# Ten of sixteen input tiles read in transposed form and normalised with broadcast rows, instead of being transposed on TensorE

## The chip, the cores and the metric

The kernel runs on one core of a Trainium2 chip. A core has five engines that run side by side: TensorE (PE in the profile, with PEld for its weight loads), VectorE (DVE), ScalarE (ACT), GpSimd (POOL) and SyncE (SP, which here only issues transfers). Each has its own instruction queue, worked off in order; they meet by semaphores. Transfers between DRAM and the on-chip memory run on 16 DMA engines, and a queue that issues one goes on at once unless the next instruction has to wait. PE writes into PSUM, eight banks of 128x512 words here. The metric is the device time of one execution in microseconds (us).

## The reference

S = 2048 rows, D = 512, F = 1792. Everything is float32.

```python
xn = layernorm(x)
# A: 32 heads of 16, each row looks at 8 rows, 2 apart, behind it
q, k, v = split(xn @ wqkv)                        # 512 -> 3*512
s = softmax(q . k[window] * 16**-0.5) @ v[window] @ wo
# B: a gated MLP with a spatial product
z = gelu(xn @ w_in)                               # 512 -> 1792
z1, z2 = z[:, :896], layernorm(z[:, 896:])
g = w_sp @ z2 + b_sp[:, None]                     # 2048 x 2048 over the rows
b = (z1 * g) @ w_out                              # 896 -> 512
out = x + s * silu(b)
```

## The kernel before

Row r of x is p*16 + j: tile j (0 to 15) holds rows p*16 + j, with p on the 128 partitions. Every matrix product is computed in three: both operands are split into a high part (fp32r, a rounded copy made by ACT) and a low part (source minus high, made by DVE), and PE adds hi·hi, hi·lo and lo·hi. So one 128x512 result over 512 channels takes 4 blocks x 3 = 12 products of 512 columns.

The stages on PE, in order:

1. Warm-up and opening. `keep_warm` (L191) multiplies the identity while the first loads run. `opening` (L196) fixes by hand the order of tiles 0 to 5: loads, layernorm statistics (`stats_x`, L160: DVE bn_stats and aggregate, plus eps, GpSimd power -1/2), normalisation (`normal_x`, L167, on rows), four PE transposes of 128x128 into one bank (`turned_x`, L170, L173), the high copy by ACT (L174) and the low part by DVE (`low_x`, L177). The normalised, transposed tile is what the qkv products read, and later z1 and z2.
2. qkv in three groups of 512 output columns, g = 0, 1, 2, each 16 tiles x 12 products (`product`, L266; in the opening `times`, L208). From tile 6 on, `layernorm_in(j + 1)` (L181) makes the next tile while tile j is multiplied. ACT copies each result into a stage buffer (L303), and a pair of tiles is written to DRAM (qkv_d, L310).
3. z1: 7 blocks of columns x 4 chunks c of rows (L398 to L410), chunk c being tiles 4c to 4c + 3; gelu by ACT at the eviction (L409), written to DRAM.
4. z2: 16 tiles x 2 halves h of 512 and 384 columns (L420 to L444), gelu (L432), layernorm statistics and split on DVE (L436, L441).
5. g: 4 chunks of rows x 16 tiles x 7 blocks (L469 to L478), with w_sp split on the way (wsp, L137); evictions with the bias and the gate z1 (L498 to L514).
6. The end: final weights wout and wo and the gated u (ul) are loaded and split (L481 to L489), then b (7 blocks, 21 products per tile) and s, and the output.

Attention (`attention`, L323) is DVE work beside PE's stages 2 to 5, in eight subs of four heads; sub 0 needs q, k, v blocks 0 to 2, which all lie in group 0. It has the lowest priority. The final weights lie in attention's memory, so their loads follow its end.

The order of each engine's instructions is made when the kernel is built, by a scheduler that plays the program through; what `pin` names is kept in the order it is written in (the opening, the weights, the layernorm of x). SP's queue holds nearly all loads, ACT's the writes of qkv, z1 and g.

Of the kernel before, what the change touches and what calls it, by code (L numbers as in the profile page):

```python
# [10 lines left out]
F32 = mybir.dt.float32  # L11
# [29 lines left out]
WARM = 10  # L41
OPEN = 6
TCKW = {"schedule_with_timeline_sim": True}
# [3 lines left out]
def kernel(  # L47
    ctx: ExitStack,
    tc: tile.TileContext,
    x: bass.AP,  # L50
    wqkv: bass.AP,
# [30 lines left out]
    g_d = dram.tile([NC - 1, FB, P, CT], F32, name="g_d")  # L82
    o_d = dram.tile([NSUB, NT, CS, P], F32, name="o_d")
# [76 lines left out]
    def stats_x(j, xt):  # L160
        st = const.tile([P, 6], F32, tag="st", name=f"st_{j}", bufs=4)
        pin(nc.vector.bn_stats(st, xt))
        pin(nc.vector.bn_aggr(mvx[:, j], st))
        pin(nc.vector.tensor_scalar(mvx[:, j, 1:2], mvx[:, j, 1:2], EPS, None, op0=ALU.add))
        pin(nc.gpsimd.tensor_tensor(mvx[:, j, 1:2], mvx[:, j, 1:2], nhalf, op=ALU.pow))

    def normal_x(j, xt):  # L167
        pin(normalise(xt, xt, mvx[:, j]))
# [27 lines left out]
    def opening(wg):  # L196
# [27 lines left out]
        high(0)  # L224
        low(0, nc.vector)
        normal_x(0, x[0])
# [4 lines left out]
        normal_x(1, x[1])  # L231
        low(1, nc.vector)
        first.append(mm("qkv_0_0"))
        keep_warm(2)
        times(0, (0, 0, 0), (0, 0, 1), (0, 1, 0))
        keep_warm(2)
        times(0, (1, 0, 0), (1, 1, 0))
        high(2)
        low(2, nc.gpsimd)
        high(3)  # L240
        p = turned_x(1, x[1])
        stats_x(2, x[2])
        low(3, nc.gpsimd)
        times(0, (2, 0, 0), (2, 1, 0), (1, 0, 1), (3, 0, 0), (3, 1, 0), (2, 0, 1))
        low_x(1, p)
        normal_x(2, x[2])
        first.append(mm("qkv_0_1"))
        times(1, *[(k, 0, 0) for k in range(KB)])
        p = turned_x(2, x[2])
        times(1, *[(k, 0, 1) for k in range(KB - 1)])  # L250
        times(0, (3, 0, 1))
        times(1, *[(k, 1, 0) for k in range(KB)], (3, 0, 1))
        for j in range(3, OPEN):
# [3 lines left out]
            normal_x(j, xt)  # L257
            first.append(mm(f"qkv_0_{j - 1}"))
# [3 lines left out]
            times(j - 1, *[(k, 1, 0) for k in range(KB)])  # L262
        low_x(OPEN - 1, p)
        pins[0] = False
# [18 lines left out]
    for g in range(NG):  # L283
        stage = None
        if g == 0:
            wg = [None] * KB
            opening(wg)
        else:
            wg = following
        for j in range(NT):  # L290
            if g == 0 and OPEN <= j + 1 < NT:
                layernorm_in(j + 1)
            if j == NT // 2 and g + 1 < NG:
                pins[0] = True
                following = [
                    prep(wqkv[:, g + 1, k, :], GC, f"wqkv_{g + 1}_{k}") for k in range(KB)
                ]
                pins[0] = False
            pq = first[j] if g == 0 and j < OPEN - 1 else product(g, j, wg)
            if j % 2 == 0:  # L300
                stage = tmp.tile([P, 2 * GC], F32, tag="t35", name=f"stage_{g}_{j}", bufs=3)
            sv = stage.rearrange("p (b j c) -> p b j c", b=NBLK, j=2)
            nc.scalar.activation(  # L303
                sv[:, :, j % 2, :], pq.rearrange("p (b c) -> p b c", b=NBLK), AF.Copy
            )
            if j % 2:
                dst = qkv_d[NBLK * g : NBLK * (g + 1), PAD:, :].rearrange(
                    "b (p j) c -> p b j c", j=NT
                )[:, :, j - 1 : j + 1, :]
                nc.scalar.dma_start(dst, sv)  # L310
# [85 lines left out]

# [193 lines left out]
```

## Time and profile before

| what | us |
|---|---|
| median of 3 runs | 731.72 (731.32 to 731.82) |
| profiled execution, its own time | 731.32 |
| its span | 729.5 |
| PE busy | 723.2 (99%) |
| DVE busy | 555.6 (76%) |
| ACT busy | 217.1 (30%) |
| DMA, mean rate over the span | 147 GB/s |

A row of the timeline shows the start, the busy time of one instruction (or of a run of xN equal ones), the engine, the line, the operation, output<-inputs, and in brackets the idle time before it and what ended that. The four transposes of a tile stand in one row (x4); a warm-up product leaves two records. A group of instructions shows busy us and mean ns after the bar, then idle time before it. A row of windows shows the stretch, its length, busy us of PE, PEld, DVE, ACT and POOL with counts, the clock granted to PE, the DMA engines' busy share and GB/s. A row of DMA issues shows how many KB one moves and the median time from issue to landing. PE's starts are the measure of its pace, since neighbouring products overlap.

### The profile page before, as it was taken

To read this page: it belongs to the slowest core of one execution; us is meant where nothing else is said; L and a number is where in the kernel's file an instruction comes from. 1 tells how busy PE (TensorE), PEld (TensorE's weight loads), DVE (VectorE), ACT (ScalarE), POOL (GpSimd) and SP (SyncE) were. 2 spreads that over 40 slices of the span, in tenths; PEclk is the share of its full clock that TensorE was granted. 3 is DMA by queue.
4 is the path that set the end of the run, shared out by engine and by line. 5 is a ranking of instruction groups with operands and counts; after the bars stand their busy time and mean duration, and the time that the engine had idled before them with its cause. 6 is when DMAs were issued, how large, how long until landed. Compare 5 with 4: busy or idle time off the path is not lost.

```text
span 729.5 us, 8846 instructions
## 1 busy us (share of the span) xinstructions
PE 723.2 (99%) x3272; PEld 604.3 (83%) x3272; DVE 555.6 (76%) x668; ACT 217.1 (30%) x339; POOL 33.0 (5%) x56
## 2 busy tenths in 40 slices
PE   8999999999999999999999999999999999999997
PEld 7888888888888889888888888888888888888886
DVE  6851999899899999998997999999996528222222
ACT  3442331342422464422131114111343514111210
POOL 3200000000000223100000000000000000000000
PEclk9999999999999999999999999999999999999999
DMA  7566577566553200433438345851288734433221
GB/s 223 158 186 195 184 230 200 182 195 196 207 145 127 84 9 13 148 101 131 135 103 286 88 127 161 258 137 58 76 293 238 225 92 147 137 92 113 89 73 43
DMA packets 108554, 107.34 MB, mean 147 GB/s; under 512 B 40288, under 2 KB 73824, under 8 KB 108512
## 3 DMA queue, kind: packets, MB, share of 16 engines
q1 hardware_dynamic: 76496, 81.22, 37.5%
q10 hardware_dynamic: 32016, 25.56, 10.8%
q8 instruction: 25, 0.41, 0.2%
q14 instruction: 17, 0.14, 0.1%
HBM read 72.88 MB, written 33.88 MB: 146 GB/s over the span
## 4 chain that ended last, share of the span: by engine, by line
PE 98%; DVE 1%; DMA 0%; ACT 0%; issue 0%; SPq 0%
PE g L477 14%; PE g L476 14%; PE g L478 14%; PE qkv L272 5%; PE qkv L274 5%; PE qkv L273 5%; PE z L429 4%; PE z L428 4%; PE z L427 4%; PE z L407 3%; PE b L521 3%; PE z L405 3%; PE b L523 3%; PE b L522 3%; PE z L406 3%; PE s L521 2%
## 5 line engine op out<-in xcount | busy, mean ns | idle before, releaser
L348 DVE TENSOR_TENSOR pr<-k,q 128x2048 f32<-128x2048 f32 x32 | 73.2, 2287 | 17.9 <-DMA q<-qkv_d 17.4
L375 DVE TENSOR_TENSOR pv<-v,lg 128x2048 f32<-128x2048 f32 x32 | 73.2, 2289 | 0.8
L351 DVE TENSOR_REDUCE lg<-pr 128x128 f32<-128x2048 f32 x32 | 73.0, 2281 | 0.6
L535 DVE TENSOR_TENSOR sg<-s,sg 128x512 f32<-128x512 f32 (+1 forms) x17 | 11.2, 660 | 78.8 <-PE s L523 78.8
L303 ACT ACTIVATE stage<-qkv 128x512 f32<-128x512 f32 x48 | 28.7, 598 | 70.4 <-PE qkv L274 66.4
L381 DVE TENSOR_TENSOR pv<-pv 128x1024 f32<-128x1024 f32 x32 | 39.0, 1220 | 0.4
L530 ACT ACTIVATE sg<-b 128x512 f32<-128x512 f32 x16 | 9.6, 597 | 65.2 <-PE b L523 65.2
L432 ACT ACTIVATE zt<-z 128x512 f32<-128x512 f32 (+1 forms) x32 | 17.3, 543 | 35.4 <-PE z L429 33.0
L409 ACT ACTIVATE z1t<-z 128x512 f32<-128x512 f32 x28 | 16.6, 594 | 36.2 <-PE z L407 31.9
L429 PE MATMUL z<-w_0h,BIG 128*128 128x512 f32 x64 | 25.2, 394 | 0.0
L428 PE MATMUL z<-w_0l,BIG 128*128 128x512 f32 x64 | 25.2, 393 | 0.0
L427 PE MATMUL z<-w_0h,BIG 128*128 128x512 f32 x64 | 24.9, 389 | 0.0
L454 DVE TENSOR_TENSOR gt<-gt,zl 128x512 f32<-128x512 f32 x28 | 18.8, 682 | 6.9 <-DMA zl<-z_d 6.9
L382 DVE TENSOR_TENSOR pv<-pv 128x512 f32<-128x512 f32 x32 | 21.8, 682 | 0.5
L429 PE MATMUL z<-w_1h,BIG 128*128 128x384 f32 x64 | 21.6, 338 | 0.0
L427 PE MATMUL z<-w_1h,BIG 128*128 128x384 f32 x64 | 21.6, 337 | 0.0
L428 PE MATMUL z<-w_1l,BIG 128*128 128x384 f32 x64 | 21.5, 336 | 0.0
L436 DVE BATCH_NORM_STATS2 zst<-zt 128x6 f32<-128x448 f32 x32 | 19.5, 612 | 1.9 <-ACT zt L432 1.7
L152 ACT ACTIVATE oh<-ol 128x512 fp32r<-128x512 f32 x16 | 10.1, 634 | 34.2 <-PE s L522 21.2
L438 POOL TENSOR_TENSOR nmz<-mvz,mone 128x1 f32<-128x1 f32 x16 | 9.0, 564 | 224.0 <-DVE mvz L437 223.9
L152 ACT ACTIVATE BIG<-ul 128x512 fp32r<-128x512 f32 x21 | 13.1, 626 | 18.6 <-PE g L477 15.2
L441 DVE SCALAR_TENSOR_TENSOR BIG<-zt,mvz,BIG 128x896 fp32r<-128x896 f32 x16 | 18.1, 1132 | 0.4
(382 smaller groups left out, 2103.0 us busy)
## 6 DMA issues: line engine op xcount, KB each, us to landing
qkv_d<-stage ACTq DMA_DIRECT2D x24, 512.0 KB, 4.3
x<-in_x SPq DMA_DIRECT2D x32, 256.0 KB, 3.8
k<-qkv_d SPq DMA_DIRECT2D x8, 960.0 KB, 5.1
v<-qkv_d SPq DMA_DIRECT2D x8, 960.0 KB, 5.2
z_d<-z1t ACTq DMA_DIRECT2D x28, 256.0 KB, 2.4
zl<-z_d SPq DMA_DIRECT2D x28, 256.0 KB, 3.6
ul<-g_d SPq DMA_DIRECT2D x21, 256.0 KB, 3.6
g_d<-gt ACTq DMA_DIRECT2D x9, 512.0 KB, 4.7
```

Of the source, the lines that this page charges most:

```text
L272: nc.tensor.matmul(pq, xh[:, c], wh, start=k == 0, stop=False)
L273: nc.tensor.matmul(pq, xh[:, c], wl, start=False, stop=False)
L348: nc.vector.tensor_tensor(pr, taps(kw, j0), qb.unsqueeze(1).to_broadcast([P, W, NJ * CS]), op=ALU.mult)
L351: nc.vector.tensor_reduce(lg[:, :, j0 * HS : (j0 + NJ) * HS], pr.rearrange("p w (i d) -> p w i d", d=DH), axis=AX.X, op=ALU.add,)
L375: nc.vector.tensor_tensor(pr.rearrange("p w (i d) -> p w i d", d=DH), taps(vw, j0).rearrange("p w (i d) -> p w i d", d=DH), lg[:, :, j0 * ...
L381: nc.vector.tensor_tensor(pr[:, 0:4], pr[:, 0:4], pr[:, 4:8], op=ALU.add)
L427: nc.tensor.matmul(pz[h][:, : WID[h]], xh[:, c], wh, start=k == 0, stop=False)
L428: nc.tensor.matmul(pz[h][:, : WID[h]], xh[:, c], wl, start=False, stop=False)
L429: nc.tensor.matmul(pz[h][:, : WID[h]], xl[:, c], wh, start=False, stop=k == KB - 1)
L476: nc.tensor.matmul(pg[f], zh[:, ff], wh, start=js == 0, stop=False)
L477: nc.tensor.matmul(pg[f], zh[:, ff], wl, start=False, stop=False)
L478: nc.tensor.matmul(pg[f], zl[:, ff], wh, start=False, stop=js == NT - 1)
```

## The change

- Tiles 6 to 15 are no longer transposed on PE. A second input x_t holds x with columns on partitions (the host only rearranges it). `row_stats(j)` loads the row tile, makes mean and rstd as before, and writes them to DRAM (mv_d, 128 partitions x 2 words). `columns(j)` loads the transposed tile (xT), loads mean and rstd back as two rows of 128 broadcast over all partitions (mr, 128x256), subtracts and multiplies on DVE (two 128x512 passes), and has ACT copy the high part from there. `low_x` then takes its low part from that tile instead of PSUM.
- Tiles 0 to 3 (JC = 4) are only freed of their mean before the transposes. Their rstd is applied at the evictions, where the row lies on a partition (scale of ACT's copy in qkv, scale of the gelu in z2), and in z1's chunk 0 by a DVE multiply with a broadcast row rb ahead of the gelu, seven times. Tiles 4 and 5 are normalised and transposed as before.
- Group 1 of the first six tiles (AHEAD = 6, 72 products) stands between group 0's tiles 5 and 6. Group 1's weights are fetched right after the opening, group 2's at group 1's tile 8.
- 8 warm-up products instead of 10, two instead of four in the opening; its first products stand in another order.
- z2 goes by pairs of tiles: half 0 of both, then half 1 of both.

```diff
-WARM = 10
+WARM = 8
 OPEN = 6
+AHEAD = 6
...
+    mv_d = dram.tile([NT, 2, P], F32, name="mv_d")
+    r_d = dram.tile([JC, P], F32, name="r_d")
...
+        if j >= JC:
+            rstd_x(j)
+
+    def rstd_x(j):
         pin(nc.vector.tensor_scalar(mvx[:, j, 1:2], mvx[:, j, 1:2], EPS, None, op0=ALU.add))
         pin(nc.gpsimd.tensor_tensor(mvx[:, j, 1:2], mvx[:, j, 1:2], nhalf, op=ALU.pow))
 
+    def late_rstd(j):
+        return mvx[:, j, 1:2] if j < JC else 1.0
+
     def normal_x(j, xt):
-        pin(normalise(xt, xt, mvx[:, j]))
+        if j < JC:
+            pin(nc.vector.tensor_scalar(xt, xt, mvx[:, j, 0:1], None, op0=ALU.subtract))
+        else:
+            pin(normalise(xt, xt, mvx[:, j]))
...
-    def layernorm_in(j):
-        xt = load_x(j)
+    def row_stats(j):
+        xt = ep.tile([P, D], F32, tag="xs", name=f"x_{j}", bufs=4)
+        nc.sync.dma_start(xt, xr[j])
         stats_x(j, xt)
-        normal_x(j, xt)
-        low_x(j, turned_x(j, xt))
+        nc.sync.dma_start(mv_d[j].rearrange("a p -> p a"), mvx[:, j])
+
+    def columns(j):
+        xt = ep.tile([P, D], F32, tag="xT", name=f"xT_{j}", bufs=3)
+        nc.sync.dma_start(xt, x_t[j])
+        mr = ep.tile([P, 2, P], F32, tag="mr", name=f"mr_{j}", bufs=4)
+        nc.sync.dma_start(
+            mr.rearrange("p a q -> p (a q)"),
+            mv_d[j].rearrange("a p -> (a p)").unsqueeze(0).to_broadcast([P, 2 * P]),
+        )
+        xv = xt.rearrange("p (k q) -> p k q", k=KB)
+        for a, op in ((0, ALU.subtract), (1, ALU.mult)):
+            pin(nc.vector.tensor_tensor(
+                xv, xv, mr[:, a].unsqueeze(1).to_broadcast([P, KB, P]), op=op
+            ))
+        pin(nc.scalar.activation(xn_at(j)[0], xt, AF.Copy))
+        return xt
...
         stats_x(0, x[0])
         high(0)
+        normal_x(0, x[0])
         low(0, nc.vector)
-        normal_x(0, x[0])
         p = turned_x(0, x[0])
...
+    order = [(0, j) for j in range(0, OPEN, 2)] + [(1, j) for j in range(0, AHEAD, 2)]
+    order += [(0, j) for j in range(OPEN, NT, 2)]
+    left = list(range(OPEN + OPEN - 3, NT))
+    ready = OPEN
+    for i, (g, j) in enumerate(order):
+        pins[0] = True
+        while ready < NT and ready < OPEN + 2 * i:
+            xt = columns(ready)
+            if ready > OPEN:
+                low_x(ready - 1, before)
+            before = xt
+            ready += 1
+            if left:
+                row_stats(left.pop(0))
...
+        pins[0] = False
+        pair(g, j)
...
+            if c == 0:
+                nc.vector.tensor_tensor(zt, pz, rb, op=ALU.mult)
+                pz = zt
             nc.scalar.activation(zt, pz, AF.Gelu_apprx_tanh)
...
+        if j % 2 == 0:
+            zts = [t35(f"zt_{i}") for i in (j, j + 1)]
+            for h in range(2):
+                for i in range(2):
+                    z2_half(j + i, h, zts[i])
```

Three places where the order of instructions differs. In the rows, the name ahead of <- is written, the names behind it are read; the last number of a name only counts buffers. The first is PE's queue at the end of the opening (xt_j is tile j's transposes, qkv_g_j the result of group g, tile j). Before:

```order
L173 MATMUL xt_5_286<-ident_79,x_5_268 128x128 x4
L210 MATMUL qkv_0_4_277<-wqkv_0_0h_133,BIG_92 128x512
L210 MATMUL qkv_0_4_277<-wqkv_0_1h_150,BIG_92 128x512
L210 MATMUL qkv_0_4_277<-wqkv_0_2h_165,BIG_92 128x512
L210 MATMUL qkv_0_4_277<-wqkv_0_3h_169,BIG_92 128x512
L173 MATMUL xt_6_315<-ident_79,x_6_307 128x128 x4
L272 MATMUL qkv_0_5_322<-wqkv_0_0h_133,BIG_92 128x512
L273 MATMUL qkv_0_5_322<-wqkv_0_0l_134,BIG_92 128x512
L173 MATMUL xt_7_345<-ident_79,x_7_337 128x128 x4
```

and in the change:

```order
L187 MATMUL xt_5_303<-ident_81,x_5_285 128x128 x4
L243 MATMUL qkv_0_4_294<-wqkv_0_0h_134,BIG_94 128x512
L243 MATMUL qkv_0_4_294<-wqkv_0_1h_149,BIG_94 128x512
L243 MATMUL qkv_0_4_294<-wqkv_0_2h_156,BIG_94 128x512
L243 MATMUL qkv_0_4_294<-wqkv_0_3h_171,BIG_94 128x512
L308 MATMUL qkv_0_5_419<-wqkv_0_0h_134,BIG_94 128x512
L309 MATMUL qkv_0_5_419<-wqkv_0_0l_135,BIG_94 128x512
L308 MATMUL qkv_1_0_467<-wqkv_1_0h_324,BIG_94 128x512
L308 MATMUL qkv_1_1_481<-wqkv_1_0h_324,BIG_94 128x512
L308 MATMUL qkv_1_2_521<-wqkv_1_0h_324,BIG_94 128x512
```

After tile 5's transposes no others follow, and products of group 1 come where those of tiles 6 and on came.

The second is SP's queue around the loads of the later tiles. Before, x's tiles stand in a row:

```order
L157 DMA x_9_397<-in_x 128x512
L157 DMA x_10_451<-in_x 128x512
L157 DMA x_11_481<-in_x 128x512
L157 DMA x_12_511<-in_x 128x512
L157 DMA x_13_541<-in_x 128x512
```

In the change, from tile 9 on (the rows of L202 are the writes of mean and rstd of tiles 9, 10 and 11):

```order
L202 DMA mv_d_78<-mvx_90 128x2x1
L208 DMA mr_9_403<-mv_d_78 128x256
L206 DMA xT_9_401<-in_x_t 128x512
L200 DMA x_14_458<-in_x 128x512
L202 DMA mv_d_78<-mvx_90 128x2x1
L206 DMA xT_10_434<-in_x_t 128x512
L200 DMA x_15_504<-in_x 128x512
L208 DMA mr_10_436<-mv_d_78 128x256
L202 DMA mv_d_78<-mvx_90 128x2x1
L206 DMA xT_11_450<-in_x_t 128x512
L208 DMA mr_11_452<-mv_d_78 128x256
```

A tile's broadcast load stands one to three issues behind the write that it reads, and the next tile's write behind that load.

The third is DVE's queue at attention's last instruction, the transpose tt_7_12 (BIG<-ul is a split of u, wsp_3 of w_sp's last chunk, gt<-g the first eviction of g's last chunk). Before:

```order
L385 STREAM_TRANSPOSE tt_7_12_1725<-pv_7_12_1720 128x256
L153 TENSOR_TENSOR BIG_92<-ul_1_2_4841,BIG_92 128x512
L137 SCALAR_TENSOR_TENSOR wsp_3_13l_4681<-wsp_3_13r_4678,mvz_89,wsp_3_13h_4680 128x512
L153 TENSOR_TENSOR BIG_92<-ul_1_3_4845,BIG_92 128x512
L153 TENSOR_TENSOR wout_0l_4766<-wout_0r_4763,wout_0h_4765 128x512
L153 TENSOR_TENSOR BIG_92<-ul_1_4_4849,BIG_92 128x512
L137 SCALAR_TENSOR_TENSOR wsp_3_14l_4708<-wsp_3_14r_4705,mvz_89,wsp_3_14h_4707 128x512
```

and in the change, from there to that eviction (wout and wo are the final weights, olo the low part of an attention output):

```order
L444 STREAM_TRANSPOSE tt_7_12_1737<-pv_7_12_1732 128x256
L157 TENSOR_TENSOR BIG_94<-ul_2_5_4903,BIG_94 128x512
L157 TENSOR_TENSOR BIG_94<-ul_2_6_4907,BIG_94 128x512
L157 TENSOR_TENSOR wout_0l_4788<-wout_0r_4785,wout_0h_4787 128x512
L157 TENSOR_TENSOR wout_1l_4794<-wout_1r_4791,wout_1h_4793 128x512
...
L157 TENSOR_TENSOR wo_3l_4932<-wo_3r_4929,wo_3h_4931 128x512
L157 TENSOR_TENSOR olo_0_4939<-ol_0_4935,oh_0_4938 128x512
L573 TENSOR_TENSOR gt_3_0_4951<-g_3_0_4342,bb_3_4949 128x512
```

Ten splits of u and the last three of w_sp stand ahead of attention's end now, two splits of u and the final weights behind it.

More of the change, by code (lines that the diff above doesn't have):

```diff
@@ L50 @@
     x: bass.AP,
+    x_t: bass.AP,
     wqkv: bass.AP,
@@ L281, with weights @@
         nc.vector.memset(mask[0:1, W - 1 - w, : DIL * w], MASKED)
[L283 to L302, printed above, removed]
+    def weights(g):
+        pins[0] = True
+        w = [prep(wqkv[:, g, k, :], GC, f"wqkv_{g}_{k}") for k in range(KB)]
+        pins[0] = False
+        return w
```

89 lines of the change are left out of this document (60 added, 29 removed).

## The prediction

> **What bounds the kernel now.** I read the busy shares first, then the chain that ended last, then the timeline of TensorE over the first 60 us, where the change works.
>
> ```profile
> PE 723.2 (99%) x3272; PEld 604.3 (83%) x3272; DVE 555.6 (76%) x668; ACT 217.1 (30%) x339; POOL 33.0 (5%) x56
> DVE  6851999899899999998997999999996528222222
> PE 98%; DVE 1%; DMA 0%; ACT 0%; issue 0%; SPq 0%
> ```
>
> TensorE (PE) is busy 99% of the 729.5 us span and makes 98% of the chain; 1.8 us of the 731.32 us lie outside the span. So an instruction taken from PE gives back its whole spacing, as long as nothing that PE waits for becomes late. The spacing is read from starts, since a busy time of 0.39 overlaps its neighbour's.
>
> ```profile
> 44.59 0.39 PE L272 MATMUL qkv<-wqkv_0h,BIG 128*128 128x512 f32 x1
> ...
> 47.08 0.39 PE L274 MATMUL qkv<-wqkv_3h,BIG 128*128 128x512 f32 x1
> 47.31 0.60 PE L173 MATMUL xt<-ident,x 128*128 128x128 f32 x4
> ```
>
> Twelve products, one tile of one group, take 47.31 - 44.59 = 2.72 us, 0.227 each.
>
> **Part 1: ten tiles lose their transposes.**
>
> ```profile
> 20.36 0.60 PE L173 MATMUL xt<-ident,x 128*128 128x128 f32 x4
> ...
> 23.62 0.60 PE L173 MATMUL xt<-ident,x 128*128 128x128 f32 x4
> ...
> 25.92 0.60 PE L173 MATMUL xt<-ident,x 128*128 128x128 f32 x4
> ...
> 28.88 0.39 PE L273 MATMUL qkv<-wqkv_0l,BIG 128*128 128x512 f32 x1
> 29.11 0.60 PE L173 MATMUL xt<-ident,x 128*128 128x128 f32 x4
> 29.47 0.47 PE L272 MATMUL qkv<-wqkv_0h,BIG 128*128 128x512 f32 x1
> 29.78 0.39 PE L273 MATMUL qkv<-wqkv_0l,BIG 128*128 128x512 f32 x1
> L173 PE MATMUL xt<-ident,x 128*128 128x128 f32 x64 | 9.7, 274 | 0.5 <-DVE x L147 0.4
> ```
>
> Between the two groups of transposes at 25.92 and 29.11 stand twelve products and 3.19 us, so four transposes cost 3.19 - 2.72 = 0.47: 0.36 until the next product starts, and that product's own step is 0.31 instead of 0.227. Ten tiles give 4.7. The pair at 20.36 and 23.62, inside the opening, has 3.26, which gives 0.54 and an upper bound of 5.4; 4.6 is the lower, for the rounding of the starts. The group's busy time (ten sixteenths of 9.7 = 6.1) is no price, since 0.60 busy stands against a step of 0.36. All 512-wide products stay.
>
> **Part 2: the opening.**
>
> ```profile
> 1.36 4.64 PE L191 MATMUL warm<-ident 128*128 128x128 f32 x20 [1.36 <-POOL ident masks.py:199]
> 6.42 0.66 PE L173 MATMUL xt<-ident,x 128*128 128x128 f32 x4 [0.43 <-DVE x L147]
> 6.92 0.61 PE L191 MATMUL warm<-ident 128*128 128x128 f32 x4
> 7.77 0.50 PE L210 MATMUL qkv<-wqkv_0h,BIG 128*128 128x512 f32 x1 [0.24 <-ACT BIG L174]
> ...
> 17.12 0.60 PE L173 MATMUL xt<-ident,x 128*128 128x128 f32 x4
> 4.88 0.15 DVE L164 TENSOR_SCALAR mvx<-mvx 128x1 f32<-128x1 f32 x1
> 5.22 0.69 DVE L204 TENSOR_TENSOR wqkv_0l<-wqkv_0r,wqkv_0h 128x512 fp32r<-128x512 f32 x1 [0.18 <-ACT wqkv_0h L200]
> 5.83 0.54 DVE L147 TENSOR_SCALAR x<-x,mvx 128x512 f32<-128x512 f32 x1
> ```
>
> PE's first transposes wait for VectorE's (DVE's) normalisation of tile 0, which stands behind the power on GpSimd and a weight split. In the change only the mean is subtracted, right where 4.88 stands: 5.83 - 4.88 = 0.95 earlier. Two of the first ten warm-ups go, and two of the four later ones (they stand where PE waits anyway), but tile 1's transposes then stand after two products instead of five and leave PE waiting some 0.6 there. I take 1.0; bounds 0 (the wait moves to tile 1) and 1.25 (0.95 and about one warm-up more).
>
> By those rows a warm-up takes 4.64/10 = 0.46 at first and 0.61/2 = 0.3 later: PE speeds up near 6 us. The Trainium skill, TensorE: Matmul & The Clock Gate, Part 1: The HAM clock gate, says the clock is halved until about one 3.4 us window of activity has passed, and that this budget is time, not a number of matmuls. The rows agree with a late flip. Eight warm-ups end near 5.07, ahead of it; by that rule the first transposes and perhaps the first products still run at half rate. That is rival D.
>
> **Part 3: what the ten tiles cost elsewhere.** Each tile j gets a second load (xT_j, 256 KB), a small write of its mean and rstd to DRAM (256 runs of 4 bytes), a broadcast load of them (mr_j, 128 KB), and two 128x512 passes on DVE in place of one normalisation.
>
> ```profile
> o_d<-tt SPq DMA_DIRECT2D x128, 32.0 KB, 2.2
> DMA to landing us min/median/max: 1.5/2.2/5.2
> bb<-in_b_sp SPq DMA_DIRECT2D x4, 256.0 KB, 4.4
> 65.00 0.42 SPq L335 DMA_DIRECT2D q<-qkv_d  x1
> x<-in_x SPq DMA_DIRECT2D x32, 256.0 KB, 3.8
> 30.00:40.00 10.00, 10.00 (x51) 8.32 (x50) 8.73 (x22) 5.43 (x10) 2.26 (x4) 1.00 0.67 192
> L179 DVE TENSOR_TENSOR BIG<-xt,BIG 128x512 fp32r<-128x512 f32 x16 | 10.9, 683 | 8.0 <-ACT BIG L174 7.9
> L147 DVE TENSOR_SCALAR x<-x,mvx 128x512 f32<-128x512 f32 x16 | 9.1, 575 | 0.9 <-POOL mvx L165 0.7
> ```
>
> (The second row belongs to the first, o_d's writes of L388; the sixth gives the window, PE, PEld, DVE, ACT, POOL, clock, DMA share and GB/s.)
>
> DVE: 2 x 0.68 - 0.58 = 0.8 a tile, 8 in all. The stretch in which the tiles are made grows by the 72 products of group 1 that now stand between tiles 5 and 6, 72 x 0.227 = 16.3, and DVE had 13% idle at its fullest. I cost DVE at nothing; with the cover gone it would be at most the 8.
>
> DMA: 3.8 MB more (ten times 384 KB) over some 45 us is 85 GB/s on top of 192 at a share of 0.67: nearly 1. By bytes alone it fits, with landings longer than before.
>
> SyncE's (SP's) queue is the real risk. From tile 9 on it holds, per tile, the write of mv_j, then mr_j, which waits for that write to land; xT, the next x row tile and later attention's k_0 stand behind. So each tile needs one round trip L plus an issue of 0.42. I place the write of mv_8 near 27.7 (two steps of 2.72 after tile 5's transposes, which come at 23.62 - 1.3 = 22.3). With four issues between, tile 9's mr issues near 29.6 + 2L, tile 15's at 29.6 + 2L + 6(L + 0.42) = 32.1 + 8L; then 4.4 to land like bb, and some 1.8 for two passes and ScalarE's (ACT's) copy: ready at 38.3 + 8L. PE wants tile 15 at about 22.3 + 0.4 + 196 products x 0.227 = 67. The write is new; its nearest rows are o_d's, also 256 small runs from SBUF to DRAM: lowest 1.5, highest 5.2, median 2.2. At 2.2 tile 15 is ready at 55.9, 11 ahead; the slack is gone at L = 3.6. I take 2.5 (o_d's median and a little for the fuller DMA), so nothing; bounds 0 and 8 x (5.2 - 3.6) = 13. Tile 6's own write and load, wanted at 42.4, start before 25 and are no closer.
>
> The Trainium skill, DMA: Bandwidth & Descriptors, Rules for kernel authors, says that a strided last dimension lowers to one descriptor per element, which speaks against mv's write; no run here shows 4-byte runs, and its sum would be part 3's with L above 2.2.
>
> **Part 4: what moves later.**
>
> ```profile
> 70.80 2.29 DVE L348 TENSOR_TENSOR pr<-k,q 128x2048 f32<-128x2048 f32 x1 [17.41 <-DMA q<-qkv_d]
> ...
> 556.40 0.45 DVE L385 STREAM_TRANSPOSE tt<-pv 128x256 f32<-128x256 f32 x1
> ...
> 563.88 0.69 DVE L153 TENSOR_TENSOR wout_0l<-wout_0r,wout_0h 128x512 fp32r<-128x512 f32 x1 [2.69 <-DMA ul<-g_d]
> ...
> 587.62 0.68 DVE L153 TENSOR_TENSOR wo_3l<-wo_3r,wo_3h 128x512 fp32r<-128x512 f32 x1
> 592.26 0.69 DVE L153 TENSOR_TENSOR olo<-ol,oh 128x512 fp32r<-128x512 f32 x1 [3.95 <-ACT oh L152]
> 596.70 0.69 DVE L153 TENSOR_TENSOR olo<-ol,oh 128x512 fp32r<-128x512 f32 x1 [3.74 <-ACT oh L152]
> 601.47 0.69 DVE L500 TENSOR_TENSOR gt<-g,bb 128x512 f32<-128x512 f32 x1 [4.08 <-PE g L478]
> 605.35 0.39 PE L521 MATMUL b<-wout_0h,BIG 128*128 128x512 f32 x1
> ```
>
> Attention is DVE work beside PE's and starts when group 0 is in DRAM. Group 0's end moves by 70 products (two of group 1 stood before it already), 15.9, less 5.7: about 10 later. Chunk 0 of z1 adds seven DVE multiplies, 7 x 0.68 = 4.8, and ten ul splits and three wsp splits now stand ahead of attention's end, 8. So its last transpose ends at 556.85 + 10 + 4.8 + 8 = 579.7, 22.8 later. Then come the final weights, which take attention's memory: before, 7 us passed to wout_0 and 23.7 from there to wo_3, and in these stood some fourteen ul and wsp splits of 0.6 to 0.7, 9 to 10. Without them 21, and with an o split and the first eviction of the last g chunk, which stand behind, 22: 602. PE's first b block ends at 605.35 - 5.7 + 21 x 0.227 = 604.4 and the second needs that eviction's bank. Spare 2.4; I cost it at nothing, bounds 0 and, at before's pace (the first o split at 592.26 + 22.8 = 615, the eviction right behind it) some 11. The second o split, at 596.70 before, stands behind that eviction now.
>
> The z1 multiplies themselves wait on DVE for at most one or two 2.29 rows; eight banks of 2.72 us each stand against that. Scaling at ACT's evictions replaces copies that exist (ACT 30% busy): nothing. Pairing z2's tiles adds nothing on PE. At its end the spatial weights take over:
>
> ```profile
> 297.53 0.75 DVE L137 SCALAR_TENSOR_TENSOR wsp_0l<-wsp_0r,mvz,wsp_0h 128x512 fp32r<-128x512 f32 x1 [0.32 <-ACT wsp_0h L136]
> 302.06 0.39 PE L477 MATMUL g<-wsp_0l,BIG 128*128 128x512 f32 x1
> ```
>
> The low half was ready at 298.28, 3.8 before PE read it. Two tiles' statistics now come in a bunch there, some 3 us of DVE work: 0, at most 1.
>
> **Sum.** 731.32 - 4.7 - 1.0 = 725.6, which is 6.1 under the median of 731.72; the profiled execution lies 0.4 under that median, so I say 725.7. The likeliest case's own range is 724.3 (5.4 and 1.25, with half a tenth of rounding) to 727.3 (4.6, 0, and part of 1 at the z2 handover).
>
> **Rivals.**
> A, the forecast, 56%: nothing new is waited for.
> B, the feed is late, 20%, the case that ends on the other side: the mv round trip on SP's queue paces tiles 9 to 15. PE stalls before one of group 0's last tiles by 8(L - 3.6). It eats the whole gain of 5.7 at L = 4.3; at 5.2, the longest o_d write, 725.6 + 13 = 739. For: DMA share near 1, the write's tiny runs, x loads of 3.8 in this stretch. Against: the median of 2.2, and what stands right ahead of a write in its queue is only a 128 KB load. I give faster 7, same 5, slower 8 of the 20.
> C, the handover at the end, 15%: attention ends after 582, and PE's second b block waits for a bank. Each us beyond costs one; 727 to 737. For: DVE is nine tenths busy through the middle, so a late start lasts to the end. Against: its row falls to six and five tenths where the final weights come, so there is room to catch up. Faster 7, same 4, slower 4.
> D, the clock, 9%: with eight warm-ups the first transposes and products run at half rate; the opening gives 0 instead of 1.0: 726.7, faster.
> That the transposes stay, or that their time was hidden, I exclude: PE has no idle row before the products that follow them.
>
> Within 0.2% (1.5 us) a measurement of this kernel can hardly tell a change. Faster: 56 + 7 + 7 + 9 = 79; same 9; slower 12. The range reaches from 724.0 to 731.0: it holds A and D but for a few, and the parts of B and C up to there, about 8 in 10.
>
> **What would show it.** Part 1: no L173 work after tile 5, and twelve products in 2.72 us throughout. Part 2: the first transposes near 5.5, the first product near 6.8, a hole before tile 1. Part 3: mr_15's issue before 58 and no PE wait on VectorE or ACT before group 0's tiles 6 to 15; if PE waits there, B. Part 4: attention's last transpose before 582 and no PE wait in b's second block; if there is one, C. The forecast is wrong if PE's idle time grows by over 1.5 us anywhere, or if the 512-wide spacing changes.

## The result, and the profile after

The change takes 797.68 us (797.38 to 799.26) against 731.62: 1.0908 of the time before, 95% interval 1.0889 to 1.0927. Forecast were 725.7 and a range to 731.0. It is 66 us slower, and all of them are lost in the first 140 us. The page of the changed kernel, whose lines answer those quoted before:

```profile
PE 732.9 (92%) x3224; PEld 608.9 (77%) x3224; DVE 567.4 (71%) x685; ACT 221.7 (28%) x341; POOL 37.4 (5%) x56
...
PE   8674354999999999999999999999999999999997
...
PEclk9977656999999999999999999999999999999999
...
PE 83%; DMA 13%; DVE 1%; SPq 1%; issue 0%; POOL 0%; ACT 0%; DVEq 0%
```

PE is busy 92% instead of 99%. From the second slice of 20 us to the seventh it is idle nearly half the time, and from the third to the seventh the clock granted to it reads 5 to 7 tenths. The chain that ended last now has 13% of transfers. What PE waited for, in all, times and longest:

```profile
PE qkv L310 <- DVE BIG L193: 44.0, 6, 15.5
PE qkv L308 <- ACT wqkv_3h L156: 12.3, 1, 12.3
```

Six times it waited for the low part of a tile made by `columns`, and once for group 1's last piece of weights. The chain between 20 and 140 us names what stood behind both (start, length, what):

```profile
20.17 14.20 DMA mv_d<-mvx
...
35.75 8.19 DMA wqkv_3r<-in_wqkv
...
48.69 11.37 DMA mv_d<-mvx
61.44 11.75 DMA mv_d<-mvx
73.62 12.13 DMA mv_d<-mvx
86.13 8.40 DMA mv_d<-mvx
94.97 11.57 DMA mv_d<-mvx
106.97 9.14 DMA mv_d<-mvx
119.14 9.38 DMA mv_d<-mvx
128.53 5.06 DMA mr<-mv_d
```

That is the write of a tile's mean and rstd, 1 KB, over and over: of tile 7, and from 48.69 on those of tiles 9 to 15 in a row, with only issues on SP between them. SP's queue shows how one is chained to the next:

```profile
60.07 0.33 SPq L208 DMA_DIRECT2D mr<-mv_d  x1
60.49 0.38 SPq L206 DMA_DIRECT2D xT<-in_x_t  x1
60.97 0.38 SPq L200 DMA_DIRECT2D x<-in_x  x1
61.44 2.45 SPq L202 DMA_DIRECT2D mv_d<-mvx  x1
63.98 0.42 SPq L206 DMA_DIRECT2D xT<-in_x_t  x1
64.50 0.38 SPq L200 DMA_DIRECT2D x<-in_x  x1
73.20 0.33 SPq L208 DMA_DIRECT2D mr<-mv_d  x1
```

From 64.9 to 73.2 SP issues nothing: mr of tile 10 waits until tile 10's write has landed, and tile 11's write stands behind it. All ten writes, from issue to landing:

```profile
DMA to landing us min/median/max: 8.4/10.6/14.2
```

The forecast had taken 2.5 for this, with 5.2 as the upper end.

### The profile page after: what moved, and what is told of

Its sections match the earlier page's. It is cut to its first block, busy times and chain, and to the rows that moved or that the text cites. A ratio compares the mean times of both kernels' runs of the same rounds, so it can differ in the third digit from the quotient of the medians.

```text
span 795.6 us, 8836 instructions
## 1 busy us (share of the span) xinstructions
PE 732.9 (92%) x3224; PEld 608.9 (77%) x3224; DVE 567.4 (71%) x685; ACT 221.7 (28%) x341; POOL 37.4 (5%) x56
## 4 chain that ended last, share of the span: by engine, by line
PE 83%; DMA 13%; DVE 1%; SPq 1%; issue 0%; POOL 0%; ACT 0%; DVEq 0%
PE g L549 13%; PE g L551 13%; PE g L550 13%; DMA mv_d<-mvx 11%; PE qkv L310 3%; PE z L496 3%; PE z L495 3%; PE qkv L308 3%; PE z L494 3%; PE qkv L309 3%; PE b L596 3%; PE z L471 3%; PE z L470 3%; PE b L594 3%; PE b L595 3%; PE z L472 3%
## 5 line engine op out<-in xcount | busy, mean ns | idle before, releaser
L407 DVE TENSOR_TENSOR pr<-k,q 128x2048 f32<-128x2048 f32 x32 | 73.2, 2286 | 1.3 <-DMA q<-qkv_d 0.9
L310 PE MATMUL qkv<-wqkv_0h,BIG 128*128 128x512 f32 x43 | 19.2, 446 | 44.0 <-DVE BIG L193 44.0
L214 DVE TENSOR_TENSOR xT<-xT,mr 128x512 f32<-128x512 f32 x20 | 13.8, 691 | 64.3 <-DMA mr<-mv_d 41.5
L310 PEld LDWEIGHTS qkv<-wqkv_0h,BIG 128*128 128x128 f32 x43 | 8.7, 202 | 48.3 <-DVE BIG L193 46.9
L330 ACT ACTIVATE stage<-qkv 128x512 f32<-128x512 f32 x36 | 21.2, 594 | 44.6 <-PE qkv L310 44.0
L308 PE MATMUL qkv<-wqkv_3h,BIG 128*128 128x512 f32 x43 | 18.8, 437 | 12.3 <-ACT wqkv_3h L156 12.3
L217 ACT ACTIVATE BIG<-xT 128x512 fp32r<-128x512 f32 x10 | 6.3, 630 | 77.0 <-DVE xT L214 76.9
L527 DVE TENSOR_TENSOR gt<-gt,zl 128x512 f32<-128x512 f32 x28 | 18.9, 687 | 10.5 <-DMA zl<-z_d 10.5
```

Of the source, the lines that this page charges most:

```text
L308: nc.tensor.matmul(pq, xh[:, c], wh, start=k == 0, stop=False)
L310: nc.tensor.matmul(pq, xl[:, c], wh, start=False, stop=k == KB - 1)
L407: nc.vector.tensor_tensor(pr, taps(kw, j0), qb.unsqueeze(1).to_broadcast([P, W, NJ * CS]), op=ALU.mult)
```

## The experiments

Theory W: the small write itself is slow, and its landing is paid once per tile on SP. Theory Q: the write waits behind other traffic. Theory M: the broadcast loads or the DVE passes pace the tiles. Each kernel below starts from the change unless it says otherwise.

**Without the writes (no_trip).**

```diff
-        nc.sync.dma_start(mv_d[j].rearrange("a p -> p a"), mvx[:, j])
...
-            mv_d[j].rearrange("a p -> (a p)").unsqueeze(0).to_broadcast([P, 2 * P]),
+            x_t[j][0, : 2 * P].unsqueeze(0).to_broadcast([P, 2 * P]),
```

> This kernel leaves the writes of mean and rstd to DRAM out; the broadcast loads of the same size and place read a row of x_t instead, so tiles 6 to 15 are scaled by wrong numbers (output not the reference's). No load waits for a write of the kernel any more. Theory W (the small write is what lasts: 8.4 to 14.2 us in the changed kernel's trace, paid once per tile on SP's queue): the forecast of 725.6 comes true, 724.3 to 727.3, and PE waits for no tile from 6 on. Theory Q (the write is short, but waits behind the added loads in full DMA queues): also near 725.6, up to 730. Theory M (the broadcast loads or the two DVE passes pace the tiles, whatever they read): stays above 760.

Measured 733.27 (1.0021 of before, 1.0011 to 1.0031). 64 of the 66 us are gone, which rules M out, but the forecast does not come true either. PE waits for no tile; one wait is left behind the opening, and the chain leads it back to r_d, the second small write (rstd of tiles 0 to 3 for z1):

```profile
PE qkv L306 <- ACT wqkv_3h L155: 3.6, 1, 3.6
```

```profile
20.39 10.13 DMA r_d<-mvx
30.55 0.32 SPq L456
30.96 0.38 SPq L199
31.43 5.01 DMA wqkv_3r<-in_wqkv
36.47 0.64 ACT wqkv_3h L155
```

SP held the last of group 1's weights back for 10 us, to load a row that DVE first reads at 153 us in this run.

**Writes that nobody reads (writes_unread).** The broadcast loads read x_t as above, the writes stay.

> The writes of mean and rstd stay, the broadcast loads read a row of x_t as in the run without the writes, so nothing waits for a write (output not the reference's). Theory W: the ten writes still hold the DMA engines, loads behind them in the same queues land some us later than without them, but no round trip is paid per tile: 726 to 745, middle 729; the writes' own landing stays at 8 or more. Theory Q: as without the writes, 725.6 to 727, and the writes land in 2 to 4 where few loads are ahead of them. Theory M: above 760.

Measured 762.38 (1.042, 1.0383 to 1.0457), above W's range. Nothing waits for one of these ten writes, and still 29 us are lost against the kernel without them; PE waits 14.5 for tiles and 6.7 for weights. The writes land in 8.0 to 17.1 (median 11.9) though nobody reads them. The loads of xT without the writes, and with them (KB each, median us to landing):

```profile
xT<-in_x_t SPq DMA_DIRECT2D x10, 256.0 KB, 4.4
```

```profile
xT<-in_x_t SPq DMA_DIRECT2D x10, 256.0 KB, 9.3
```

So the write does two kinds of harm. Taken apart in this order, some 29 us come from slowing the loads around it, and the other 35 from the round trips.

**Half as many runs, of 8 bytes (runs8).** mv_d is laid out [NT, P, 2].

```diff
-        nc.sync.dma_start(mv_d[j].rearrange("a p -> p a"), mvx[:, j])
+        nc.sync.dma_start(mv_d[j], mvx[:, j])
...
-                xv, xv, mr[:, a].unsqueeze(1).to_broadcast([P, KB, P]), op=op
+                xv, xv, mr[:, :, a].unsqueeze(1).to_broadcast([P, KB, P]), op=op
```

> Mean and rstd of a row lie side by side in DRAM, so a tile's write has 128 runs of 8 bytes instead of 256 of 4; the broadcast load has the same bytes, and the DVE passes read it with a step of 2. All else as in the change. Theory W with a price per run: the write lands in about half, 4 to 7, and the feed shortens by 8 x 5 = 40: 750 to 762. Theory Q, or a price per write whatever its runs: 790 to 800. A price that goes by bytes written to one line of DRAM rather than by runs: also no change.

Measured 755.58 (1.0337, 1.0324 to 1.0351), as W with a price per run said; its writes land so:

```profile
DMA to landing us min/median/max: 4.5/6.0/11.1
```

The median falls from 10.6 to 6.0 with the bytes unchanged. The runs are half as many here and also twice as long, so this alone does not say which of the two counts.

**Runs of 128 bytes (dve_turn).** DVE turns mean and rstd into rows first, in a tile of 32 columns.

```diff
-        nc.sync.dma_start(mv_d[j].rearrange("a p -> p a"), mvx[:, j])
+        pin(nc.vector.transpose(tr, mvw[:, j - OPEN]))
+        for a in range(2):
+            nc.sync.dma_start(
+                mv_d[j, a].rearrange("(b q) -> b q", q=Q),
+                tr.rearrange("(b r) q -> b r q", r=Q)[:, a],
+            )
```

> Mean and rstd of a tile are turned by DVE (a 128x32 transpose in blocks of 32) into rows of 32 words and written by two transfers of four runs of 128 bytes; one more small DVE instruction and one more issue per tile. All else as in the change, and the result is that of the reference. Theory W: the write lands in 1.5 to 3.5 like the attention outputs' 128-byte runs, tile 15 is ready near 56 to 66, and the forecast comes true: 725 to 728. Theory Q: the write still lands in 8 or more behind the same loads: above 780. Theory M: above 760.

Measured 738.15 (1.0102, 1.0085 to 1.0118). W's direction, not its number: the transposes on DVE cost 0.21 each, mr now issues 2 to 4 us after its write, and PE's waits for tiles fall from 44.0 to 3.8; the wait of 3.7 for weights, r_d's, is still there.

**Neither trip (no_trips).** As no_trip, and rb reads x_t as well.

> As the run without the writes of mean and rstd, and the second small write, r_d (512 runs of 4 bytes, read back as rb for z1), is left out too: rb reads a row of x_t, so the output is not the reference's. In the run before this one SP waited from 20.4 to 30.5 us for r_d to land, the last piece of group 1's weights stood behind it, and PE waited 3.6 us for that piece and then ran some ten products at 0.43 instead of 0.227. Theory S (these two trips are all that the sum missed): PE waits for nothing after tile 1, and 730.1 + 1.8 - 3.6 - 2 = 726, between 725.0 and 727.3. Rival R (the opening's full DMA queues, 356 GB/s from 10 to 20 us, hold the weights back anyway): a wait of 2 us or more stays before the first products of group 1, 729 to 733.

Measured 727.33 (0.9951, 0.9937 to 0.9964), theory S: faster than before, inside the forecast's own range. Rows of DVE and PE near the end:

```profile
579.83 0.45 DVE L441 STREAM_TRANSPOSE tt<-pv 128x256 f32<-128x256 f32 x1
...
601.14 1.28 DVE L569 TENSOR_TENSOR gt<-g,bb 128x512 f32<-128x512 f32 x2
600.69 0.39 PE L590 MATMUL b<-wout_0h,BIG 128*128 128x512 f32 x1
```

These bear on part 4 of the forecast; more on them below.

**r_d alone left out (no_rb).** The ten trips stay.

```diff
-    nc.sync.dma_start(r_d.rearrange("j p -> p j"), mvx[:, :JC, 1])
...
-        rb, r_d.rearrange("j p -> (j p)").unsqueeze(0).to_broadcast([P, CT])
+        rb, x_t[0][0, :].unsqueeze(0).to_broadcast([P, CT])
```

> The change with r_d's write left out and rb read from a row of x_t (output not the reference's); the ten writes of mean and rstd and their round trips stay. It gives r_d's share. SP's wait for tile 7's write (34.4 in the change) and the nine trips of 8 to 12 behind it stay, 512 runs fewer stand ahead of tile 7's write: 4 to 8 less, 789 to 794. If r_d's wait at 30 were what delays the whole chain: under 785.

Measured 795.77 (1.0883, 1.0866 to 1.0899): 1.9 less than the change, under the 4 to 8 expected, and the two intervals overlap. r_d costs 5 to 6 where it stands alone (no_trip against no_trips, by the ratios and by the medians); behind the other trips its cost is not clear of the noise.

**The order of the code on SP (pinned).** The four transfers are kept in the order they are written in.

```diff
-        nc.sync.dma_start(xt, x_t[j])
+        pin(nc.sync.dma_start(xt, x_t[j]))
```

> The change with one thing altered: the transfers of the row tiles, of the columns, and of mean and rstd are kept in the order of the code on SP, so that the broadcast load of tile j stands behind the write of tile j + 2 instead of right behind its own. The writes have 256 runs of 4 bytes as in the change. Theory W (the write's landing of about 10 us, serialised once per tile by the order on SP): three round trips overlap, and a chain of 18 us (broadcast load 5, passes 1.3, statistics and power 1.6, write 10) makes three tiles: 6 a tile instead of 12, tile 15 some 34 late, 755 to 775. Rival T (the traffic of the small runs holds the DMA engines, whatever the order): 785 to 800.

Measured 821.19 (1.123, 1.1213 to 1.1247): outside both theories' ranges. The round trip is indeed overlapped, since mr of tile j now stands behind the write of tile j + 2; but it is issued 0.9 behind that write, with xT's load between, and lands late without waiting for anything. From its chain:

```profile
44.39 11.39 DMA mr<-mv_d
55.88 0.70 DVE xT L214
...
60.85 11.46 DMA mr<-mv_d
```

A load of 128 KB takes 11.4 behind a small write in its queue (median of the ten mr 11.0, of xT 11.0, of x 10.9). It is not that full DMA engines slow it: from 45.95 to 47.7 the engines move nothing at all, though mr, xT and x are issued by then, and of their 0.64 MB SP's queue moves 0.45 after the write has landed, at 52.4. And each such load stands behind a write that needs the passes of the tile before, so one tile takes 16.5 (44.39 to 60.85), and the three trips of my count never run side by side. The same order with 128-byte runs (turn_pin, r_d late as in turn_late below):

> The same as the run with r_d late, and the transfers kept in the order of the code on SP as in the run that pins them; the result is that of the reference. With writes that land in 3, one chain of broadcast load 5, passes 1.3, statistics and power 1.6 and write 3 makes three tiles in 11, 3.6 a tile, against 2.72 that PE wants; from 32 at tile 6 tile 15 is ready near 67, as PE wants it. Theory S: 725 to 730, no better than without the order, since a short write gains little by being overlapped. Rival R: 730 to 735.

Measured 766.16 (1.0474, 1.046 to 1.0488), outside both theories' ranges and, as it seems, for that second reason alone: from the second on, each mr of its chain lands in 3 to 4, and a tile takes 9.

**The small writes on ACT's queue (act_queue).**

```diff
-        nc.sync.dma_start(mv_d[j].rearrange("a p -> p a"), mvx[:, j])
+        nc.scalar.dma_start(mv_d[j].rearrange("a p -> p a"), mvx[:, j])
```

> The change with the writes of mean and rstd issued by ACT instead of SP, still 256 runs of 4 bytes. Theory H (in the run with the pinned order a broadcast load that waits for nothing took 11 right behind a write in SP's queue: the small runs block what stands behind them in the same queue): the loads on SP land in 3 to 5, the writes overlap, three tiles take 10 + 5 + 3 = 18, tile 15 is some 30 late: 755 to 770. Theory E (the small runs hold the engines themselves, whatever the queue): the loads still land in 8 to 11, 785 or more.

Measured 768.45 (1.0506, 1.0487 to 1.0525). H's time, but not all of H: xT and mr still land in 7.8 and 7.5 (median), not in 3 to 5. The writes, median 10.2, slow loads of the other queue too. The Trainium skill, DMA: Bandwidth & Descriptors, Rules for kernel authors, says that spreading transfers over issuing engines does not help, since all run on the same 16 DMA engines; with a median of 7.5 for mr there against 11.0 in pinned, where write and load share a queue, this run agrees in part.

**What makes the write slow (probe, probe2).** The kernel before, with eight unread writes in z2; they differ in length and distance of their runs, 128 but for the first of probe. Each row below is a single write. DMA is nearly idle beside the second to the fifth write; beside the last two of each run its share is 0.5, since w_sp's loads have begun.

```diff
+        if j % 2:
+            probe(j // 2, mv)
```

> The kernel before, with eight writes to DRAM that nobody reads, one behind every second tile of z2, where the DMA engines are nearly idle (share 0.04 to 0.25 in the kernel before); a 128-partition tile is written in runs of different length. Theory P (each run shorter than some size costs an engine about 0.55 us, 16 engines share the runs): 256 runs of 4 bytes land in 8 to 10; 128 runs of 8, of 4 side by side and of 4 bytes 512 apart in 4 to 6 each; from some length on (32 to 128 bytes) in about 2. Theory N (it is neighbours in one line of DRAM that hinder each other): the 128 runs of 4 bytes 512 apart land in about 2, those side by side in 4 to 6. Theory Q (traffic): all land in about 2 here.

> The kernel before with eight other unread writes at the same places of z2: 128 runs of 4 bytes at distances of 8, 16, 32, 64 and 4 bytes, then 128 runs of 8 and of 16 bytes side by side, then 8-byte runs 32 bytes apart. In the run before, 128 runs landed in 7.5 (4 bytes side by side), 4.0 (8 side by side), 1.5 (32 side by side) and 1.5 (4 bytes 512 apart). Theory N32 (runs that fall into the same 32 bytes wait for each other, 1.5 + 0.86 for each further one): 4.1, 2.4, 1.5, 1.5, 7.5, 4.1, 2.4, 1.5. Theory N64 (the same with 64 bytes, 0.4 for each further one): 4.1, 2.7, 1.9, 1.5, 7.5, 4.1, 2.7, 1.9. Theory P (a price per short run): all 4 to 8.

| runs, bytes, distance in DRAM | us to landing |
|---|---|
| 256 of 4, side by side | 7.7 |
| 128 of 4, side by side | 7.5 and 7.4 |
| 128 of 4, 8 bytes apart | 2.7 |
| 128 of 4, 16 / 32 / 64 / 512 apart | 1.4 / 1.9 / 1.5 / 1.5 |
| 128 of 8, side by side | 4.0 and 3.0 |
| 128 of 32 / 64, side by side | 1.5 / 1.5 |
| beside w_sp's loads: 128 of 16, side by side | 2.2 |
| beside w_sp's loads: 128 of 128 / 256, side by side | 2.5 / 2.6 |
| beside w_sp's loads: 128 of 8, 32 apart | 2.6 |

The two that tell most, the third and the fourth write of probe:

```profile
DMA to landing us min/median/max: 7.5/7.5/7.5
...
DMA to landing us min/median/max: 1.5/1.5/1.5
```

They have the same number of runs, the same 4 bytes, and the same idle engines; one writes them side by side, the other 512 bytes apart. And 256 runs in two such rows take 7.7, hardly more than 128 in one. So neither the length of a run nor their number makes the landing long (P falls, and so does Q here), but how close they lie in DRAM (N). Nor is it that one DMA engine carries them all. The engines' row from 260.5 to 272.3, 0.295 us a digit, with SP's queue below it (packets, MB, share), shows the third write, issued at 260.9 and landed 7.5 later:

```profile
DMA  0010200000000000000000006000000000000000
q1 hardware_dynamic: 144, 0.00, 0.7%
```

Its packets stand in the fifth digit, and 0.7% of 16 engines' 11.8 us is 1.3 us in all; the other two digits are loads of instructions. What lasts comes behind the engines' own work. Within how many bytes is not settled: 16 apart lands in 1.4, 32 apart in 1.9, two equal writes differ by up to 1.0 (4.0 and 3.0), and the formulas for 32 and 64 bytes both missed the 2.7 at 8 apart and the 1.4 at 16. The Trainium skill, Collectives: The Full Stack, Rules for kernel authors, has the buffers of collectives aligned to 32 bytes, which prevents the hardware from reading, modifying and writing. These rows fit that in part, since two runs in 32 bytes, 16 apart, cost nothing more; no run shows what the memory does.

**The same in place (runs32).** As runs8, each row padded to 32 bytes; the broadcast load grows to 512 KB.

> As the run with 8-byte runs, each row's mean and rstd now padded to 32 bytes (128 runs of 32 bytes side by side), no run sharing 32 bytes with another; the broadcast load grows from 128 to 512 KB a tile, and DVE reads it with a step of 8. r_d keeps its 4-byte runs. Theory N: the write lands in 2 to 4 in place of 6.0 (median of the 8-byte runs), as many runs as there; the time is then set by the larger loads and by r_d's wait, 735 to 752. Theory P: the write stays at 4.5 to 11, the time above 755.

Measured 747.83 (1.0224, 1.0205 to 1.0242). With four times the bytes to write and to load it is 7.8 faster than runs8:

```profile
DMA to landing us min/median/max: 1.4/4.5/11.8
```

The shortest landing falls from 4.5 to 1.4, the level of the probes. The median only goes from 6.0 to 4.5, above N's 2 to 4: N decides in an idle place; that the writes queue here behind the larger loads (Q) would explain the rest and is not shown apart. r_d's 4-byte runs are still there.

**The mended version (turn_late, turn_buf, turn_more, turn_act, turn_buf4, turn_buf6).** dve_turn, with r_d turned the same way and made behind the last tile (turn_late):

```diff
-    nc.sync.dma_start(r_d.rearrange("j p -> p j"), mvx[:, :JC, 1])
...
+    pin(nc.vector.tensor_copy(r4[:, :JC], mvx[:, :JC, 1]))
+    pin(nc.vector.transpose(t4, r4))
+    for i in range(JC):
+        nc.sync.dma_start(
+            r_d[i].rearrange("(b q) -> b q", q=Q),
+            t4.rearrange("(b r) q -> b r q", r=Q)[:, i],
+        )
```

> The run with mean and rstd turned by DVE into 128-byte runs, and r_d made the same way (one more 128x32 transpose, four transfers of four runs of 128 bytes) behind the last of the ten tiles instead of at 19 us; the result is that of the reference. Theory S: SP is free for group 1's weights from 20 to 30, the waits of 3.7 us before group 1 and of 3.8 us in all before tiles 11 to 15 go: 725 to 728. Rival R: a wait for weights or for tiles of 2 us or more stays: 730 to 735.

Measured 730.22 (0.9988, 0.9979 to 0.9997). The wait for weights is gone; waits of 0.5 to 1.95 for tiles are left. S missed, and the time is in R's range. With six buffers for xT (turn_buf):

```diff
-        xt = ep.tile([P, D], F32, tag="xT", name=f"xT_{j}", bufs=3)
+        xt = ep.tile([P, D], F32, tag="xT", name=f"xT_{j}", bufs=6)
```

> The run with r_d late and 128-byte runs, with six buffers for the transposed tiles instead of three, so that their loads need not wait in SP's queue behind the broadcast loads' waits; the result is that of the reference. In the run before it PE waited 0.5, 1.25 and 1.95 us before tiles 13 to 15, and VectorE ahead of them for xT. Theory S: these waits go, 726 to 728. Rival R: the broadcast loads then end last, 729 to 731.

Measured 729.16 (0.9973, 0.9963 to 0.9983), in R's range, and faster than both kernels, though by 0.3% only than the one before. What PE waited for in turn_late, and in turn_buf:

```profile
PE qkv L324 <- DVE BIG L194: 3.7, 3, 1.9
```

```profile
PE qkv L324 <- DVE BIG L194: 2.8, 4, 1.1
...
PE qkv L257 <- ACT BIG L189: 1.3, 2, 1.1
```

The waits for tiles shrink and one in the opening comes up, as the added loads fall there. Group 1's tiles 6 and 7 between group 0's 7 and 8 (turn_more):

> As the run with six buffers, and group 1's tiles 6 and 7 stand between group 0's tiles 7 and 8, so that tiles 8 to 15 are wanted 24 products, 5.4 us, later; attention starts 5.4 later. The result is that of the reference. Theory S: no wait is left for a tile, and if the end has the room, 725 to 727. Rival C of the forecast: attention ends too late, and PE waits for a bank in b's second block, 727 to 735.

Measured 733.25 (1.0022, 1.0012 to 1.0032). No wait for a tile is left, and the end is late, as in the forecast's rival C, but at another place: attention's last transpose ends at 587.7, past C's 582, and PE waits for the high copy of the first o tile in s, which ACT makes behind the final weights, and not for a bank in b.

```profile
PE s L617 <- ACT oh L156: 3.1, 1, 3.1
```

The writes on ACT's queue (turn_act), and four buffers beside six (turn_buf4, turn_buf6):

> The run with 128-byte runs, r_d late and six buffers, the writes of mean and rstd issued by ACT, so that they don't stand behind the loads in SP's queue; the result is that of the reference. In the run before it PE waited 2.8 in four times for tiles and 1.1 for tile 3's copy. Theory S: a write lands in 2 instead of 3 to 4, the waits for tiles go, 726 to 728.5. Rival: ACT, which waits in order for DVE's turn before each write, hands the high copies over later, 729 to 732.

> The mended version with four buffers for the transposed tiles: one of their loads fewer than with six falls into the opening. With six, tile 4's transposes came at 20.43 instead of 19.31 with three, and the waits for tiles fell from 3.7 to 2.8. Theory (both are the same DMA time, moved): the opening as with three (tile 5's transposes near 22.8) and waits of some 3 for tiles, 728 to 730. If four are enough for both: 726 to 728. The result is that of the reference.

> The mended version with six buffers once more, beside the one with four on the same chip: 728.5 to 730, 0.2% to 0.4% under the kernel before, as in the run with six before.

turn_act measured 733.62 (1.0032, 1.0021 to 1.0044): waits for ACT's copies rise from 1.3 to 2.3 and those for tiles to 3.8, as the rival had it, at a time above its 732. turn_buf4 measured 729.77 (0.998, 0.9971 to 0.9988), turn_buf6, the same kernel as turn_buf, 729.23 (0.9973, 0.9964 to 0.9982). Four and six buffers differ by less than these intervals can tell.

## Why the prediction was wrong

**Part 1, ten tiles at 0.47, was right.** From tile 5's transposes to the end of the span the kernel before takes 729.5 - 23.62 = 705.9; no_trips, with its transposes at 24.11, takes 725.1 - 24.11 = 701.0. That is 4.9 against 4.7.

**Part 2 was right in the change, and D did not come.** The opening of the changed kernel:

```profile
5.23 1.09 PE L187 MATMUL xt<-ident,x 128*128 128x128 f32 x4
...
7.01 0.50 PE L243 MATMUL qkv<-wqkv_0h,BIG 128*128 128x512 f32 x1 [0.24 <-ACT BIG L188]
...
22.50 0.60 PE L187 MATMUL xt<-ident,x 128*128 128x128 f32 x4
```

Tile 5's transposes come 23.62 - 22.50 = 1.1 earlier; 1.0 was forecast. The first four transposes do run slowly, 1.09 instead of 0.66, but the first products don't. In no_trips the gain is lost:

```profile
24.11 0.60 PE L185 MATMUL xt<-ident,x 128*128 128x128 f32 x4
```

Tile 5 comes 0.5 later than before there, since PE waits 1.5 for tile 3's high copy, for which ACT stands idle until a transfer has landed. That is where most of the 1.6 between 727.3 and the forecast went. Traffic alone does not decide it: from 10 to 20 us no_trips has 359 GB/s, and dve_turn, with tile 5 at 22.65, has 357.

**The step that failed is part 3's "I take 2.5".** The mechanism was named as rival B: the round trip on SP's queue paces tiles 9 to 15. Only its size was off, by a factor of four: the trip measured 10.5, the mean of tiles 9 to 15. I took o_d's row as the nearest because it has 256 runs as well, and gave its longest, 5.2, as the upper end; what the row did not share was that the runs start 4 bytes apart, where o_d's are 128 bytes long, and that decided. The formula comes near: with 10.5, 38.3 + 8L is 122, and tile 15 was ready at 136. Of the other 14, 9.5 lie ahead of tile 9: its mr issued at 60.07, where 29.6 + 2L gives 50.6, because the weights stood behind a wait too, and DVE, in order, split them before it made tile 9's statistics. Some 3 are issues between the later trips, and 1 is behind the last. The sentence on the skill's rule, one descriptor for each element, pointed to this write, and I gave it no weight, since no row had a price for it. The probes show that the number of runs is not the price, though: as many of 4 bytes land in 1.5 when they lie 512 apart. A price of "at least o_d's" with no upper end from the trace would have been honest, and the range then wider.

**Two things were not in the sum at all.** Of what stands on SP behind the wait of a broadcast load I named xT, x and k_0, and overlooked group 1's last weights; they stood behind mr_7's, which was issued at 34.38, and made the first wait, 12.3. And r_d's own write and wait were not costed; alone it is 5 to 6.

**The stall is dearer than its length.** PE waited 56.3 in the seven waits, but the change lies 71.8 over the sum (797.4 - 725.6). After a wait the changed kernel's products stand 0.43 apart:

```profile
135.76 0.80 PE L310 MATMUL qkv<-wqkv_0h,BIG 128*128 128x512 f32 x1 [5.56 <-DVE BIG L193]
136.36 0.63 PE L308 MATMUL qkv<-wqkv_1h,BIG 128*128 128x512 f32 x1
136.78 0.63 PE L309 MATMUL qkv<-wqkv_1l,BIG 128*128 128x512 f32 x1
...
139.33 0.40 PE L309 MATMUL qkv<-wqkv_3l,BIG 128*128 128x512 f32 x1
139.57 0.40 PE L310 MATMUL qkv<-wqkv_3h,BIG 128*128 128x512 f32 x1
```

Eight products take 3.57 instead of 1.82, 1.75 more. Over all steps between starts, the products behind each of the seven waits take 1.8 to 3.0 longer than at 0.227, 15.8 in all; 56.3 + 15.8 = 72.1, which is the 71.8.

**Part 4 was right.** Attention's last transpose was forecast to end at 579.7 and the first eviction of the last g chunk at 602; with the feed in time (no_trips) they came at 580.3 and 601.1, and PE did not wait. The 579.7 is partly luck: attention began 12.8 later than before (83.56 against 70.80) instead of 10, and lost 10.7 from there instead of 12.8. How narrow it is shows in turn_more, where attention starts 3.3 later than in turn_buf (91.00 against 87.71) and PE waits 3.1.

**Two slips of the sum** are small beside this. 725.6 was worked out from the profiled 731.32; carried over to the median, 0.4 higher, it is 726.0 and not 725.7. And 5.4, 1.25 and half a tenth off 731.32 leave 724.6, not 724.3.

## What to carry to other kernels

A write of words side by side, one from each partition, was here not a small transfer but a slow one, and it slowed the loads behind it: turn the words into rows of 32 on the chip first (738.15 for 797.68), or leave room between them, which made the load of them four times as large here (747.83). Where a load waits for a write of the same kernel on an in-order queue, list everything that stands behind that wait, and put a trip whose result is wanted late behind what is wanted soon. A new kind of transfer without a row of its own has no upper end in the rows of others; before a change rests on it, it is worth one write in a quiet place.

## What the runs showed of the hardware

- A write of 128 runs of 4 bytes lands in 7.5 when they lie side by side in DRAM, and in 1.5 when they lie 512 bytes apart (probe); at 32 and 64 bytes a run, side by side costs nothing (1.5).
- A load of 128 KB that waits for nothing takes 11.0 (median) behind such a write of 256 runs in the same queue (pinned), and 7.5 when the write is in another queue (act_queue). Why a write that keeps the engines busy only briefly (1.3 us in all for 128 runs, probe) holds up loads for so long, in pinned even while the engines stand idle, stays open.
- After a wait PE's pace can halve for some 3 us, from 0.227 to 0.43 a product, at a granted clock of 0.50. Waits of 2.36 and 2.73 (runs32), 3.07 (turn_more), 3.17 (the change) and 3.60 (no_trip) did it; of shorter ones 1.76 (act_queue) and 2.19 (runs32) did, 1.95 (turn_late) and 2.03 (dve_turn) did not. The Trainium skill, TensorE: Matmul & The Clock Gate, Part 1: The HAM clock gate, has the clock fall back to half after an idle window of about 3.4 us; here shorter waits were enough, and the measurement decides.
